# Top-k over folded pairs, and normalisation moved to POOL, in an attention and GELU kernel

## The chip, the cores and the metric

The kernel runs on one core of a Trainium2 chip. The metric is the device time of one launch in microseconds, the median of the runs shown. A core has five engines that matter here, each with its own in-order queue of instructions: PE (TensorE, matrix multiplication), DVE (VectorE), ACT (ScalarE), POOL (GpSimd) and SP, which issues most transfers. The engines wait for one another by semaphores; within one engine the order is the order in which the program emits the instructions.

## What is computed

```python
# q, k, v: (8, 8, 576, 64), w_in: (512, 2048), w_out: (2048, 512), all float32
scores = matmul(q, k.transpose(0, 1, 3, 2)) / sqrt(64)
kth    = np.partition(scores, -32, axis=-1)[..., -32:-31]      # the 32nd largest of a row
scores = np.where(scores >= kth, scores, -1e9)
scores = scores - max(scores, axis=-1)
attn   = exp(scores);  attn = attn / (sum(attn, axis=-1) + 1e-9)
x      = matmul(attn, v)              # brought to (4608, 512): tokens x heads*64
h      = x @ w_in                     # 4608 x 2048
out    = (0.5 * h * (1 + erf(h / sqrt(2)))) @ w_out
```

## The kernel before

**Items.** The 64 heads are taken in pairs (32 pairs), and the rows of a pair in blocks of 128. An item is one block of two rows of scores a partition: `s` is 128 x 1152, two rows of 576 scores (`e` = 0 and 1). Blocks 0 to 3 of a head give one item each, and the last 64 rows of two pairs share an item. There are N = 144 items, 18 a batch.

**The loop.** Iteration n of the main loop (L662) works on several items at once, each a stage further: the scores of item n + 2 (L668: matmuls on PE at L290 and L294, copied out by ACT at L304 and L305), the top-k of item n (L721, on DVE), the softmax of item n - 1 (ACT, L386 and L387), the transposes of item n - 2 (PE, L418 and L436, copied by ACT) and the product with v of item n - 3 (L473). Between them stand pieces of the two large products, at most eight an iteration and four in iterations 10 and 11 (`left`, L664): L525 is the product with w_in, L536 the GELU on ACT, L561 the product with w_out.

**Top-k.** `top_k` (L332) finds the 32 largest of each row on DVE in four rounds. A round takes the eight largest (L347, `max`), and, except the last, replaces these eight by the lowest number (L350, `match_replace`), for both rows in turn. That is 8 maxima and 6 replacements over 576 numbers an item. After the last round a hook runs: the DVE transposes of q and k of a later pair where one is due (L255; each lets SP load that buffer's next pair, six transfers for q and six for k), and `inverse` of item n - 1 (L373, a reciprocal of the softmax sum).

**Threshold and softmax.** `threshold` (L357) is two small POOL operations behind the end of top-k. ACT lowers what is below the 32nd value (Prelu with a steep slope) and exponentiates, summing into `den`. `add_small` (L379) on POOL adds 1e-9 when both rows of item n - 1 are done. `normalise` (L392) multiplies the rows of item n - 1 by `rden`. It is emitted behind the threshold of item n, so it is behind it in POOL's queue. In the iterations where the weights of the next slot are finished by POOL (`on_pool`, slots after START = 10 whose words are already loaded), both multiplications run on DVE instead.

**Weights.** The weights arrive as halves of 64-bit numbers and are put together into float32 in 16 units of 128 x 1024, one in each of the slots 1 to 10 and 13 to 18. `weights_size` makes two or three ACT passes (L190, L192, L194). `weights_add` and `weights_end` are POOL additions (L213, L225), in the late slots with a POOL scaling ahead of them (L210). Most units are staged in the part of `w_out_sb` that is not filled yet, four of them in a pool of their own (`stage`, tile `words`).

**Other names.** `xT` holds the attention output transposed, as a ring of 1152 tokens (`RING`), four groups of features. `keep_busy` (L636) puts matmuls without a use on PE in the first ten iterations. `load` (L88) brings one pair of q, k or v: for q and k six transfers, four of them of the 64 or 72 KB kind and two of the 8 KB kind for the last 64 rows of the second head. Before the loop, L112 to L114 load pair 0 (k from ACT's queue, q from SP's), L628 to L631 load pair 1 and the first weights from SP's queue, and L642 to L647 transpose pairs 0 and 1 on DVE and issue the scores of items 0 and 1.

Of the kernel before, what the change touches and what calls it, by code (L numbers as in the profile page):

```python
# [8 lines left out]
TOPK = 32  # L9
LOWEST = -3.4028234e38  # L10
# [4 lines left out]
def kernel(  # L15
# [69 lines left out]
    def raw_of(n, pair):  # L85
        return raws[n][pair % len(raws[n])]

    def load(n, pair, queue=None, queue2=None):  # L88
        if pair >= n_pairs:
            return  # L90
        queue = queue or nc.sync
        queue2 = queue2 or queue
        b, h0 = pair // NP, 2 * (pair % NP)
        t, src = raw_of(n, pair), sources[n]
        if n != "v":
            for e, a in ((0, 0), (0, 1), (1, 0), (1, 1)):
                at = e * D + a * SQ
                for lo, hi, c in ((0, S, 0),) if e == 0 else ((0, SM, 0), (SM, S, SM + TL)):
                    (queue if a == 0 else queue2).dma_start(  # L99
                        out=t[at : at + SQ, c : c + hi - lo].rearrange("p (j d) -> p j d", d=SQ),  # L100
                        in_=src[b, h0 + e, lo:hi, a * SQ : (a + 1) * SQ].rearrange(
                            "(j p) d -> p j d", p=SQ
                        ),
                    )
            return
        for e in range(2):
            queue.dma_start(
                out=t[:, 0:NM, e, :], in_=src[b, h0 + e, 0:SM].rearrange("(t p) d -> p t d", p=P)
            )
            queue2.dma_start(out=t[e * TL : (e + 1) * TL, NM, e, :], in_=src[b, h0 + e, SM:S])  # L110

    load("k", 0, nc.scalar)  # L112
    load("q", 0)
    make_identity(nc, ident)  # L114


# [36 lines left out]
    def load_weights(n, queue=None):  # L153

        queue = queue or nc.sync
        u = unit_in(n)
        if u is None:
            return
        src, r, c, dst = weights_of(u)
        if src.dtype == f32:  # L160
            for x in range(2):
                queue.dma_start(
                    out=dst[:, x], in_=src[(r + x) * P : (r + x + 1) * P, c : c + WS]
                )
            return


        half, i = src.bitcast(u16), ORDER.index(u)
        if i not in (2, 12, 14, 15):
            at = FT // 2 + 4 * (i % 2)  # L170
            t = w_out_sb[:, at : at + 4, :].rearrange("p (a b) n -> p a (b n)", a=2)
        else:
            t = stage.tile([P, 2, 2 * WS], f32, tag="words", name="words")
        for a in range(2):
            queue.dma_start(
                out=t[:, a].bitcast(u16)[:, 0 : 4 * WS - 1],
                in_=half[(r + a) * P : (r + a + 1) * P, 4 * c + 1 : 4 * (c + WS)],
            )
        words[u] = t

    def parts(u):

        t, dst = words[u], weights_of(u)[3].bitcast(i32)
        return t[:, :, 0::2], t.bitcast(mybir.dt.int16)[:, :, 2::4], t[:, :, 1::2].bitcast(i32), dst

    def weights_size(u):
        if u not in words:
# [12 lines left out]
    def waits(u):  # L200

        return u == ORDER[-1]
# [3 lines left out]
    def weights_add(u):  # L206
        if u in words:
            w, _, below, d = parts(u)
            if on_pool(u):
                nc.gpsimd.tensor_scalar(  # L210
                    w.bitcast(i32), w.bitcast(u32), 2.0**-13, None, op0=ALU.mult
                )
            nc.gpsimd.tensor_tensor(d, d, below, op=ALU.add)  # L213
            if not ends_late(u):
                weights_end(u)
        made.add(u)
# [33 lines left out]
    def transpose_qk(pair):  # L250

        def piece(x, n):
            if pair not in qk_of:
                qk_of[pair] = work.tile([P, 2 * QK], f32, tag="qk", bufs=NP + 2, name="qk")
            nc.vector.transpose(qk_of[pair][:, x * QK : (x + 1) * QK], raw_of(n, pair))  # L255
            load(n, pair + 2)

        return [lambda x=x, n=n: piece(x, n) for x, n in ((1, "k"), (0, "q"))]
# [5 lines left out]
    def row(i, e):  # L264
        return S_of[i][:, e * S : (e + 1) * S]
# [14 lines left out]
    def scores(i):  # L280
# [25 lines left out]
        else:  # L306
# [22 lines left out]
                func=AF.Copy, scale=scale,  # L329
            )  # L330

    def top_k(i, hooks):  # L332


        stat_of[i] = st = {
            "top": work.tile([P, 2, TOPK], f32, tag="top", name="top"),
            "neg": work.tile([P, 2, 2], f32, tag="neg", name="neg"),
            "bias": work.tile([P, 2], f32, tag="bias", name="bias"),
            "den": work.tile([P, 2], f32, tag="den", name="den"),
            "rden": work.tile([P, 2], f32, tag="rden", name="rden"),  # L340
        }
        cur = [row(i, e) for e in range(2)]
        rest = work.tile([P, 2, S], f32, tag="rest", bufs=1, name="rest")
        n_op = 0
        for r in range(TOPK // 8):
            for e in range(2):
                nc.vector.max(st["top"][:, e, 8 * r : 8 * r + 8], cur[e])  # L347
            if r < TOPK // 8 - 1:
                for e in range(2):
                    nc.vector.match_replace(  # L350
                        rest[:, e], st["top"][:, e, 8 * r : 8 * r + 8], cur[e], LOWEST
                    )
                cur = [rest[:, e] for e in range(2)]
            if r in hooks:
                hooks.pop(r)()

    def threshold(i):  # L357

# [30 lines left out]
            accum_out=st["den"][:, e : e + 1],  # L389
        )  # L390

    def normalise(i, on_dve):  # L392

        if i < 0 or i >= N:
            return
        st = stat_of[i]
        for e in range(2):
            s = row(i, e)
            (nc.vector if e >= 2 - on_dve else nc.gpsimd).tensor_scalar(  # L399
                s, s, st["rden"][:, e : e + 1], None, op0=ALU.mult  # L400
            )

    pt_now = [None]
# [218 lines left out]
    ready, left = [0], [0]  # L622

    eager = [False]
    staging = ExitStack()
    stage = staging.enter_context(tc.tile_pool(name="stage", bufs=1))

    load("k", 1)  # L628
    load("q", 1)
    for n in range(1, 3):  # L630
        load_weights(n)  # L631
# [7 lines left out]
            nc.tensor.matmul(warm[:, 0:P], lhsT=m, rhs=m, start=True, stop=True)  # L639

    keep_busy(WARM, idle)
    for pair in range(2):  # L642
        for piece in transpose_qk(pair):
            piece()
        if pair == 0:
            scores(0)
            scores(1)  # L647

# [11 lines left out]
    for n in range(ahead):  # L662

        left[0] = 4 if n in (START, START + 1) else 8  # L664
        eager[0] = n > N
        if not waits(unit_in(n)):
            weights_add(unit_in(n))
        scores(n + 2)  # L668
        product = attend(n - 3)
        late = n > START  # L670
        if n <= START:

            softmax(n - 1, 0)
        copy_x()
        if waits(unit_in(n)):
            weights_size(unit_in(n))
            weights_add(unit_in(n))
        mlp(1)
        tr = transposes(n - 2)
        if product and n > START and done[0] < len(pieces) and pieces[done[0]][0] > ready[0]:  # L680

            for piece in tr[:1]:
                piece()
            tr, ready[0] = tr[1:], n_tok[0]
        if n > START:
            softmax(n - 1, 0)
        mlp(1)
        if not late:
            softmax(n - 1, 1)
        mlp(1)  # L690
        if n < START:

            keep_busy((4 if product or n == 0 else 14) * (1 if n < 5 else 2), ident)
        for piece in tr[:-1]:
            piece()
            if n < START and product and piece is tr[0]:
                keep_busy(5 if n < 5 else 10, ident)
            ready[0] = n_tok[0]
            mlp(1)
        ready[0] = n_tok[0]  # L700
        if late:
            softmax(n - 1, 1)
        add_small(n - 1)
        if ends_late(unit_in(n)):
            weights_end(unit_in(n))
        for piece in tr[-1:]:
            piece()
            mlp(1)
        if n == 1:
            keep_busy(8, ident)  # L710

        run_gelus()
        mlp(left[0])
        run_gelus()
        if n < N:
            def behind_searches():
                for piece in prep_in.pop(n, []):
                    piece()
                inverse(n - 1)

            top_k(n, {3: behind_searches})  # L721
        else:
            inverse(n - 1)
        threshold(n)
        u = unit_in(n + 1)

        normalise(n - 1, 2 if on_pool(u) else 0)

        if not waits(unit_in(n + 1)):
            weights_size(unit_in(n + 1))  # L730
        for m in (n + 1, n + 2):

            if m > 2 and waits(unit_in(m)) == (m == n + 1):
                load_weights(m)
        if n <= NP:
            load("v", n)

    ready[0], left[0] = NT, len(pieces)
    while done[0] < len(pieces):
        mlp(1)  # L740
        run_gelus()
    staging.close()


# [30 lines left out]
```

## Time and profile before

| | us |
|---|---|
| median of 3 runs | 1621.87 (1621.77 to 1622.47) |
| the profiled execution: its own time | 1622.63 |
| its span, first to last instruction | 1620.9 |
| mean granted TensorE clock | 0.987 |
| ACT busy | 1144.1 |
| POOL busy | 663.9 |

The span is what the profile covers; the run's own time is 1.73 us more. PE's busy time is modelled from pipelined matmuls, so a busy PE is not PE at its peak. What an edit is worth depends on the engine that sets the pace at that place, which the chain of waits shows: it starts from the last instruction and goes back, at each step, to what released it.

Single groups that the change touches, from the groups by shape (busy time in us and mean in ns; x is the count):

```profile
L350 DVE MATCH_REPLACE8 rest<-top,rest 128x576 f32<-128x576 f32 x576 | 423.2, 742 | 0.0
L350 DVE MATCH_VALUE_LOAD rest<-top,rest 128x8 f32 x576 | 44.2, 77 | 0.0
L373 DVE RECIPROCAL rden<-den 128x2 f32<-128x2 f32 x144 | 21.6, 150 | 75.1 <-POOL den L379 74.9
L379 POOL TENSOR_SCALAR den<-den 128x2 f32<-128x2 f32 x144 | 32.1, 223 | 785.2 <-ACT s L387 784.8
L399 DVE TENSOR_SCALAR s<-s,rden 128x576 f32<-128x576 f32 x10 | 7.0, 741 | 0.3
```

The last column is the idle time of the engine before these instructions and what ended it. A replacement is two instructions, the load of its eight values and the pass itself.

### The profile page before, as it was taken

To read this page: it belongs to the slowest core of one execution; us is meant where nothing else is said; L and a number is where in the kernel's file an instruction comes from. 1 tells how busy PE (TensorE), PEld (TensorE's weight loads), DVE (VectorE), ACT (ScalarE), POOL (GpSimd) and SP (SyncE) were. 2 spreads that over 40 slices of the span, in tenths; PEclk is the share of its full clock that TensorE was granted. 3 is DMA by queue.
4 is the path that set the end of the run, shared out by engine and by line. 5 is a ranking of instruction groups with operands and counts; after the bars stand their busy time and mean duration, and the time that the engine had idled before them with its cause. 6 is when DMAs were issued, how large, how long until landed. Compare 5 with 4: busy or idle time off the path is not lost.

```text
span 1620.9 us, 25358 instructions
## 1 busy us (share of the span) xinstructions
PE 1588.7 (98%) x8864; PEld 1082.8 (67%) x8864; DVE 1460.1 (90%) x3108; ACT 1144.1 (71%) x2038; POOL 663.9 (41%) x758
## 2 busy tenths in 40 slices
PE   6899899999999999999999999999999999999999
PEld 5676476766666667776666667676666666666665
DVE  7999999999999999999999998999999999999800
ACT  4898787777777777777777777777777777777720
POOL 3886754333444333344333344333344333444400
PEclk7999999999999999999999999999999999999999
DMA  6533320011101211012100111002110101000000
GB/s 138 169 93 93 92 58 1 20 32 36 35 1 32 33 24 29 1 29 44 36 16 16 29 30 43 1 21 37 30 36 8 36 1 36 2 14 7 1 13 13
DMA packets 202640, 56.18 MB, mean 35 GB/s; under 512 B 193680, under 2 KB 193936, under 8 KB 202512
## 3 DMA queue, kind: packets, MB, share of 16 engines
q1 hardware_dynamic: 199968, 54.13, 14.5%
q8 instruction: 70, 1.15, 0.3%
q10 hardware_dynamic: 2544, 0.43, 0.1%
q14 instruction: 58, 0.48, 0.1%
HBM read 45.08 MB, written 9.44 MB: 34 GB/s over the span
## 4 chain that ended last, share of the span: by engine, by line
PE 87%; DVE 10%; DMA 1%; SPq 1%; issue 0%; POOL 0%; ACT 0%; DVEq 0%; ACTq 0%; POOLq 0%
PE y_ps L561 30%; PE h_ps L525 30%; PE o L473 8%; PE s_ps L294 7%; PE tp L436 7%; DVE top L347 5%; DVE rest L350 4%; PE t_ps L290 2%; PE o L484 1%; PE tp_t L418 1%; PE s_ps L321 1%; SPq L99 1%; DVE qk L255 1%; DVE s L399 0%; PE t_ps L310 0%
## 5 line engine op out<-in xcount | busy, mean ns | idle before, releaser
L347 DVE MAX8 top<-rest 128x8 f32<-128x576 f32 x864 | 609.2, 746 | 0.0
L525 PE MATMUL h_ps<-xT,w_in_sb 128*128 128x256 f32 (+1 forms) x2560 | 547.5, 361 | 0.0
L561 PE MATMUL y_ps<-w_out_sb,g 128*128 128x512 f32 x1152 | 545.0, 600 | 0.0
L399 POOL TENSOR_SCALAR s<-s,rden 128x576 f32<-128x576 f32 x278 | 477.1, 1726 | 8.6 <-DVE rden L373 8.0
L525 PEld LDWEIGHTS h_ps<-xT,w_in_sb 128*128 128x128 f32 x2560 | 432.7, 191 | 64.2 <-issue 14.8
L350 DVE MATCH_REPLACE8 rest<-top,rest 128x576 f32<-128x576 f32 x576 | 423.2, 742 | 0.0
L379 POOL TENSOR_SCALAR den<-den 128x2 f32<-128x2 f32 x144 | 32.1, 223 | 785.2 <-ACT s L387 784.8
L561 PEld LDWEIGHTS y_ps<-w_out_sb,g 128*128 128x128 f32 x1152 | 198.8, 191 | 187.0 <-issue 186.2
L304 ACT ACTIVATE s<-s_ps 128x1024 f32<-128x1024 f32 x127 | 130.7, 1029 | 177.4 <-PE s_ps L294 177.0
L387 ACT ACTIVATE s<-s,bias 128x576 f32<-128x576 f32 x288 | 223.3, 776 | 12.6
L386 ACT ACTIVATE s<-s,neg 128x576 f32<-128x576 f32 x288 | 224.1, 778 | 0.5 <-POOL neg L362 0.4
L443 ACT COPY pt<-tp 128x512 f32<-128x512 f32 x256 | 147.1, 575 | 101.9 <-PE tp L436 101.3
L350 DVE MATCH_REPLACE8 rest<-top,s 128x576 f32<-128x576 f32 x288 | 211.6, 742 | 0.0
L436 PEld LDWEIGHTS tp<-ident,s 128*128 128x128 f32 x1152 | 143.5, 142 | 89.3 <-issue 57.6
L347 DVE MAX8 top<-s 128x8 f32<-128x576 f32 x288 | 201.5, 741 | 0.0
L436 PE MATMUL tp<-ident,s 128*128 128x128 f32 x1152 | 174.2, 275 | 3.9 <-ACT pt L419 3.5
L473 PE MATMUL o<-pt,raw_v 128*64 128x256 f32 x1280 | 152.9, 385 | 0.5 <-ACT pt L443 0.5
L294 PE MATMUL s_ps<-qk 64*128 64x256 f32 x1024 | 150.8, 414 | 0.9 <-ACT s L302 0.5
L473 PEld LDWEIGHTS o<-pt,raw_v 128*64 128x64 f32 x1280 | 86.5, 137 | 64.5 <-issue 15.1
L294 PEld LDWEIGHTS s_ps<-qk 64*128 64x128 f32 x1024 | 91.1, 192 | 23.6 <-ACT s L302 0.8
L536 ACT ACTIVATE g<-h_ps 128x512 f32<-128x512 f32 x144 | 78.6, 594 | 37.8 <-PE h_ps L525 37.1
L387 ACT ACT_TABLE_LOAD x67 | 86.0, 1283 | 5.1
(72 smaller groups left out, 1002.9 us busy)
## 6 DMA issues: line engine op xcount, KB each, us to landing
raw_v<-in_v_dram SPq DMA_DIRECT2D x64, 128.0 KB, 2.4
out_dram<-y SPq DMA_DIRECT2D x31, 256.0 KB, 2.2
w_out_sb<-in_moe_w_in_dram SPq DMA_DIRECT2D x14, 511.8 KB, 4.9
w_out_sb<-in_moe_w_out_dram SPq DMA_DIRECT2D x10, 511.8 KB, 4.1
raw_q<-in_q_dram SPq DMA_DIRECT2D x64, 72.0 KB, 2.2
raw_k<-in_k_dram SPq DMA_DIRECT2D x62, 72.0 KB, 2.3
raw_q<-in_q_dram SPq DMA_DIRECT2D x64, 64.0 KB, 2.2
raw_k<-in_k_dram SPq DMA_DIRECT2D x62, 64.0 KB, 2.2
```

The costliest lines, as they stand in the source:

```text
L294: nc.tensor.matmul(s_ps[:, e, c * 256 : (c + 1) * 256], lhsT=lhsT[rows, :], rhs=qk[rows, KM + c * 256 : KM + (c + 1) * 256], start=True, s ...
L304: nc.scalar.activation(spread(s, S + TL, SM), s_ps, func=AF.Copy, scale=scale)
L347: nc.vector.max(st["top"][:, e, 8 * r : 8 * r + 8], cur[e])
L350: nc.vector.match_replace(rest[:, e], st["top"][:, e, 8 * r : 8 * r + 8], cur[e], LOWEST)
L386: nc.scalar.activation(s, s, func=AF.Prelu, bias=st["neg"][:, e, 1:2], scale=1.0, alpha=STEEP)
L387: nc.scalar.activation(s, s, func=AF.Exp, bias=st["bias"][:, e : e + 1], scale=1.0, accum_out=st["den"][:, e : e + 1],)
L399: (nc.vector if e >= 2 - on_dve else nc.gpsimd).tensor_scalar(s, s, st["rden"][:, e : e + 1], None, op0=ALU.mult)
L436: nc.tensor.transpose(tp[:, j * P : (j + 1) * P], s[:, first + j * P : first + (j + 1) * P], ident)
L443: nc.scalar.copy(out=dst, in_=tp.rearrange("p (j n) -> p j n", j=NM))
L473: nc.tensor.matmul(o[e * D : (e + 1) * D, 0:n], lhsT=vt[:, j, e, :], rhs=pt[:, e * NM + j if j < NM else 2 * NM, :], start=(j == 0), stop= ...
L525: nc.tensor.matmul(h_tile(u)[:, i, :], lhsT=w_in_sb[:, ko, f * P : (f + 1) * P], rhs=xT[:, ko, c0 : c0 + n], start=(ko == 0), stop=(ko == ...
L561: nc.tensor.matmul(y_of[sub], lhsT=g_of[u][:, i, sub * P : (sub + 1) * P], rhs=w_out_sb[:, f, :], start=(f == 0), stop=(f == FT - 1),)
```

## The change

- **Top-k over pairs.** `fold` splits a row of 576 into two halves of 288 and takes element by element the larger (`high_of`) and the smaller (`low_of`). The smaller is a DVE minimum up to item 19 (`BY_POOL` = 20). From item 20 it is made on POOL from the bit patterns as integers: sum of both, less the larger. A smaller number can be among the 32 largest only if its partner is, so at most 16 of the 32 come from `low_of`. `top_k` searches the 32 largest of `high_of` (four rounds) and, from the third round, the 16 largest of `low_of` (two rounds), in place. With a_1 to a_32 and b_1 to b_16 falling, the 32nd of both together is the largest over j = 0 to 16 of min(a_(32-j), b_j), with b_0 the greatest number: one minimum over 2 x 17 with one list read backwards, and one reduction.
- **When the fold runs.** Up to item 19 the fold of item n + 1 follows the top-k of item n on DVE. From item 20 it stands at the head of iteration n, on DVE and POOL. Item 0 is folded right before its search.
- **Normalisation** is always on POOL, as multiplication by `rden` and a second one by 1.0. The POOL scaling of the weights (L210) gets a second multiplication by 1.0 as well.
- **First loads.** For pair 0 the two transfers of the last rows go to POOL's queue, for k and for q (`for_tail`), and k of pair 1 goes to ACT's queue. The DVE transposes of pair 1 move from before the loop into the hook behind the first round of item 0's search; the scores of item 2 move behind that search.
- **Staging.** The pool `stage` is gone; its four units are staged in the last 512 tokens of `xT`, in four transfers instead of two.

```diff
-    load("k", 0, nc.scalar)
-    load("q", 0)
+    load("k", 0, nc.scalar, nc.gpsimd)
+    load("q", 0, None, nc.gpsimd)
...
-            t = stage.tile([P, 2, 2 * WS], f32, tag="words", name="words")
-        for a in range(2):
+            t = xT[:, :, RING - WS :]
+        n = 4 * WS // (t.shape[1] // 2)
+        for a in range(t.shape[1]):
...
-                    w.bitcast(i32), w.bitcast(u32), 2.0**-13, None, op0=ALU.mult
+                    w.bitcast(i32), w.bitcast(u32), 2.0**-13, 1.0, op0=ALU.mult, op1=ALU.mult
...
+    def fold(i):
+        if i >= N:
+            return
+        two = S_of[i].rearrange("p (e h n) -> p h e n", e=2, h=2)
+        high_of, low_of = HL_of[i] = [
+            work.tile([P, 2, S // 2], f32, tag=t, name=t) for t in ("high_of", "low_of")
+        ]
+        a, b, hi, lo = (t.bitcast(i32) for t in (two[:, 0], two[:, 1], high_of, low_of))
+        nc.vector.tensor_tensor(high_of, two[:, 0], two[:, 1], op=ALU.max)
+        if i < BY_POOL:
+            nc.vector.tensor_tensor(low_of, two[:, 0], two[:, 1], op=ALU.min)
+            return
+        nc.gpsimd.tensor_tensor(lo, a, b, op=ALU.add)
+        nc.gpsimd.tensor_tensor(lo, lo, hi, op=ALU.subtract)
...
+        def round_of(x, dst, last):
+            for e in range(2):
+                nc.vector.max(dst[:, e], x[:, e])
+            if not last:
+                for e in range(2):
+                    nc.vector.match_replace(x[:, e], dst[:, e], x[:, e], LOWEST)
         for r in range(TOPK // 8):
+            round_of(high_of, top[:, :, 8 * r : 8 * r + 8], r == TOPK // 8 - 1)
+            if r >= TOPK // 16:
+                x = r - TOPK // 16
+                round_of(low_of, low_top[:, :, 8 * x + 1 : 8 * x + 9], r == TOPK // 8 - 1)
             if r in hooks:
                 hooks.pop(r)()
...
+        nc.vector.tensor_tensor(both, rising, low_top, op=ALU.min)
+        nc.vector.tensor_reduce(
+            top[:, :, TOPK - 1 : TOPK], both, axis=mybir.AxisListType.X, op=ALU.max
+        )
...
-            (nc.vector if e >= 2 - on_dve else nc.gpsimd).tensor_scalar(
-                s, s, st["rden"][:, e : e + 1], None, op0=ALU.mult
+            nc.gpsimd.tensor_scalar(
+                s, s, st["rden"][:, e : e + 1], 1.0, op0=ALU.mult, op1=ALU.mult
             )
...
-    load("k", 1)
+    load("k", 1, nc.scalar)
...
-    for pair in range(2):
-        for piece in transpose_qk(pair):
-            piece()
-        if pair == 0:
-            scores(0)
-            scores(1)
+    for piece in transpose_qk(0):
+        piece()
+    scores(0)
+    scores(1)
...
+        if n + 1 >= BY_POOL:
+            fold(n + 1)
...
-        scores(n + 2)
+        if n > 0:
+            scores(n + 2)
...
-            top_k(n, {3: behind_searches})
+            hooks = {3: behind_searches}
+            if n == 0:
+                fold(0)
+                hooks[0] = lambda: [piece() for piece in transpose_qk(1)]
+            top_k(n, hooks)
+            if n == 0:
+                scores(2)
+            if n + 1 < BY_POOL:
+                fold(n + 1)
...
-        normalise(n - 1, 2 if on_pool(u) else 0)
+        normalise(n - 1)
```

More of the change, by code (lines that the diff above doesn't have):

```diff
@@ L86, in raw_of, with load @@
         return raws[n][pair % len(raws[n])]
-    def load(n, pair, queue=None, queue2=None):
+    def load(n, pair, queue=None, for_tail=None):
         if pair >= n_pairs:
@@ L91, in load @@
         queue = queue or nc.sync
-        queue2 = queue2 or queue
+        for_tail = for_tail or queue
         b, h0 = pair // NP, 2 * (pair % NP)
@@ L98, in load @@
                 for lo, hi, c in ((0, S, 0),) if e == 0 else ((0, SM, 0), (SM, S, SM + TL)):
-                    (queue if a == 0 else queue2).dma_start(
+                    (for_tail if lo else queue).dma_start(
                         out=t[at : at + SQ, c : c + hi - lo].rearrange("p (j d) -> p j d", d=SQ),
@@ L109, in load @@
             )
-            queue2.dma_start(out=t[e * TL : (e + 1) * TL, NM, e, :], in_=src[b, h0 + e, SM:S])
-    load("k", 0, nc.scalar)
-    load("q", 0)
+            queue.dma_start(out=t[e * TL : (e + 1) * TL, NM, e, :], in_=src[b, h0 + e, SM:S])
+    load("k", 0, nc.scalar, nc.gpsimd)
+    load("q", 0, None, nc.gpsimd)
     make_identity(nc, ident)
@@ L172, in load_weights @@
         else:
-            t = stage.tile([P, 2, 2 * WS], f32, tag="words", name="words")
-        for a in range(2):
+            t = xT[:, :, RING - WS :]
+        n = 4 * WS // (t.shape[1] // 2)
+        for a in range(t.shape[1]):
+            row, at = divmod(a * n, 4 * WS)
+            end = min(at + n, 4 * WS - 1)
             queue.dma_start(
-                out=t[:, a].bitcast(u16)[:, 0 : 4 * WS - 1],
-                in_=half[(r + a) * P : (r + a + 1) * P, 4 * c + 1 : 4 * (c + WS)],
+                out=t[:, a].bitcast(u16)[:, 0 : end - at],
+                in_=half[(r + row) * P : (r + row + 1) * P, 4 * c + 1 + at : 4 * c + 1 + end],
             )
@@ L183, in parts @@
         t, dst = words[u], weights_of(u)[3].bitcast(i32)
-        return t[:, :, 0::2], t.bitcast(mybir.dt.int16)[:, :, 2::4], t[:, :, 1::2].bitcast(i32), dst
+        if t.shape[1] == 4:
+            t = t.rearrange("p (a b) n -> p a b n", a=2)
+            dst = dst.rearrange("p a (b n) -> p a b n", b=2)
+        return t[..., 0::2], t.bitcast(mybir.dt.int16)[..., 2::4], t[..., 1::2].bitcast(i32), dst
     def weights_size(u):
@@ L330, in scores @@
             )
+    HL_of = {}
+    HALF = TOPK // 2
+    BY_POOL = 2 * START
+    low_tops = [const.tile([P, 2, HALF + 1], f32, name=f"low_top{x}") for x in range(2)]
+    for t in low_tops:
+        nc.vector.memset(t[:, :, 0:1], -LOWEST)
+    def fold(i):
[12 more added lines that the diff above has]
+        nc.gpsimd.tensor_tensor(lo, lo, hi, op=ALU.subtract)
     def top_k(i, hooks):
@@ L341, in top_k @@
         }
-        cur = [row(i, e) for e in range(2)]
-        rest = work.tile([P, 2, S], f32, tag="rest", bufs=1, name="rest")
-        n_op = 0
-        for r in range(TOPK // 8):
[L346 to L353, printed above, removed]
+        top, low_top, (high_of, low_of) = st["top"], low_tops[i % 2], HL_of.pop(i)
+        def round_of(x, dst, last):
[4 more added lines that the diff above has]
+                    nc.vector.match_replace(x[:, e], dst[:, e], x[:, e], LOWEST)
+        for r in range(TOPK // 8):
+            round_of(high_of, top[:, :, 8 * r : 8 * r + 8], r == TOPK // 8 - 1)
+            if r >= TOPK // 16:
+                x = r - TOPK // 16
+                round_of(low_of, low_top[:, :, 8 * x + 1 : 8 * x + 9], r == TOPK // 8 - 1)
             if r in hooks:
                 hooks.pop(r)()
+        both = work.tile([P, 2, HALF + 1], f32, tag="both", bufs=1, name="both")
+        falling = top[:, :, HALF - 1 :]
+        rising = bass.AP(
+            tensor=falling.tensor, offset=falling.offset + HALF,
+            ap=[list(falling.ap[0]), list(falling.ap[1]), [-1, HALF + 1]],
+        )
+        nc.vector.tensor_tensor(both, rising, low_top, op=ALU.min)
+        nc.vector.tensor_reduce(
+            top[:, :, TOPK - 1 : TOPK], both, axis=mybir.AxisListType.X, op=ALU.max
+        )
     def threshold(i):
@@ L390, in softmax, with normalise @@
         )
-    def normalise(i, on_dve):
+    def normalise(i):
         if i < 0 or i >= N:
@@ L624 @@
     eager = [False]
-    staging = ExitStack()
-    stage = staging.enter_context(tc.tile_pool(name="stage", bufs=1))
-    load("k", 1)
+    load("k", 1, nc.scalar)
     load("q", 1)
@@ L741 @@
         run_gelus()
-    staging.close()
 _INS = ["q", "k", "v", "moe_w_in", "moe_w_out"]
```

## The prediction

> **What bounds the kernel now.** I read four views in this order: busy times and slices, the chain of waits from the start to 260 us, the windows of single items, and the groups by shape with a close timeline.
>
> ```profile
> span 1620.9 us, 25358 instructions
> PE 1588.7 (98%) x8864; PEld 1082.8 (67%) x8864; DVE 1460.1 (90%) x3108; ACT 1144.1 (71%) x2038; POOL 663.9 (41%) x758
> PE   6899899999999999999999999999999999999999
> DVE  7999999999999999999999998999999999999800
> ```
>
> PE and DVE both look full, so shares settle nothing; the order in time does.
>
> ```profile
> 10.49 1.77 DMA raw_q<-in_q_dram
> ...
> 13.16 1.37 DVE top L347 x2
> 14.53 1.46 DVE rest L350 x2
> 15.98 1.32 DVE top L347 x2
> ...
> 145.20 1.65 DVE s L399 x2
> ...
> 191.68 0.74 DVE qk L255
> 192.48 0.48 PE t_ps L310 x4
> ```
>
> The chain is DVE from 13.16 to 192.4 us (items 0 to 16) and PE without a gap from there to the end. Matmul work after 192 us is not touched, so only what shortens or lengthens items 0 to 16 moves the end. An item begins where its first maximum begins: 13.16, 23.60, 34.01, 44.36, 54.86, 64.57 and so on; 9.71 us when nothing else is on DVE. Two maxima start 1.32 apart and two replacements 1.46, so an instruction costs 0.66 and 0.73, and 8 x 0.66 + 6 x 0.73 = 9.66, plus 0.05 for the reciprocal.
>
> ```profile
> 83.97:93.67 9.70, 9.61 (x83) 8.44 (x81) 9.70 (x23) 9.38 (x15) 9.29 (x8) 1.00 0.35 111
> 134.66:146.85 12.19, 12.19 (x68) 9.31 (x65) 12.08 (x25) 11.98 (x21) 5.95 (x6) 1.00 0.49 119
> 169.83:182.03 12.20, 11.97 (x67) 6.72 (x67) 12.16 (x26) 8.15 (x12) 8.41 (x7) 1.00 0.55 135
> ```
>
> Columns: window and its length, then busy time of PE, weight load, DVE, ACT and POOL with counts. Up to item 10 ACT (9.38 of 9.70) and POOL (9.29) stand just behind DVE: a faster DVE alone wins at most 0.3 us an item there. Items 12 to 16 last 12.19, 10.77, 12.21, 12.20 and 12.17 us, together 59.5, against 10.76 that PE needs for an item when it sets the pace (score matmuls at 238.66 and 249.42 us in the chain).
>
> **The change, part by part.**
>
> *Searches on 288.* The 8-value load before a replacement takes 0.067, a 576 maximum 0.66, so 0.593 / 568 = 1.04 ns an element. At 288 a maximum is 0.66 - 0.30 = 0.36 and a replacement 0.43. There are now 12 and 8: 4.32 + 3.44 = 7.76. The fold adds a maximum and, up to item 19, a minimum over 576 pairs in all; the nearest row is the 576 maximum, so 2 x 0.66 = 1.32. The closing minimum over 34 and the reduction are like the reciprocal (0.15 for 2 elements) plus 34 ns, each waiting for the one before: 0.43. Sum 7.76 + 1.32 + 0.43 + 0.05 = 9.56 against 9.71: 0.15 us an item, nearly nothing. From item 20 the minimum is POOL's and DVE saves 0.8, but PE sets the pace there, so I cost that at nothing. POOL's two integer operations on 576 are 2 x 1.35 (128x1024 took 2.41) = 2.7 us, hidden in the wait of POOL for ACT before its small addition (784.8 us in 139 times, 5.6 each); with that cover gone an item could lose up to 2.7 less DVE's 0.8.
>
> *Contention of the fold with POOL.* No two-input DVE operation exists before. The nearest rows are the ten normalisations on DVE, which meet POOL:
>
> ```profile
> 180.16 2.94 POOL L210 TENSOR_SCALAR w_out_sb<-w_out_sb 128x1024 int32<-128x1024 uint32 x1
> 180.31 1.72 DVE L399 TENSOR_SCALAR s<-s,rden 128x576 f32<-128x576 f32 x2
> 156.67 0.95 DVE L399 TENSOR_SCALAR s<-s,rden 128x576 f32<-128x576 f32 x2
> ```
>
> Where POOL was already running, the pair took 1.72; where DVE came first, 0.95 (POOL's next operation then took 3.23 instead of 2.95). So a stall is worth 0.78 for DVE; bounds per item 0 and 2 x 0.78 = 1.56. The fold starts right behind the reduction on which POOL's threshold waits, so DVE comes first: I take 0.2. Items 1 to 11: (0.2 - 0.15) x 11 = +0.6; ends -1.7 and +15.5.
> The Trainium skill, "SBUF — State Buffer", section "Who interferes with whom", speaks against this part: an instruction with two SBUF inputs contends with a GpSimd instruction that reads, and the loser blocks fully. By the rule a late fold would wait out a whole normalisation of 1.73 us, near +17 us over these 11 items; the pair of 1.72 us finished while POOL's 2.94 ran on, which is less than that.
>
> *Normalisation.* DVE loses ten instructions in items 12 to 16: 1.65 + 0.95 + 1.01 + 1.72 + 1.69 = 7.0 us. POOL gets them, and all carry a second multiplication, as does the weight scaling.
>
> ```profile
> L399 POOL TENSOR_SCALAR s<-s,rden 128x576 f32<-128x576 f32 x278 | 477.1, 1726 | 8.6 <-DVE rden L373 8.0 <-PE o L473 0.4
> L213 POOL TENSOR_TENSOR w_in_sb<-w_in_sb,w_out_sb 128x1024 int32<-128x1024 int32 x7 | 16.9, 2411 | 0.2
> masks.py:199 POOL TENSOR_SCALAR_AFFINE_SELECT ident<-ident 128x128 f32<-128x128 f32 x1 | 0.3, 293 | 0.1
> ```
>
> A one-multiplication pass costs (1726 - 223) / 574 = 2.6 ns an element (223 is the 128x2 row), more than the two-input addition at 2.1; the affine select, with two computations, costs (293 - 223) / 126 = 0.56. So the slow row is not bound by reading. Bounds for two multiplications on 576: 0.54 by the select, 3.2 by twice the present work. I take 1.1, midway between the select and the present row, since in having both operations filled the select is nearer and in everything else the present row is. The scaling on 1024 then goes from 2.95 to about 1.9.
> The Trainium skill, "GPSIMD Engine Reference", section "Elementwise — side-by-side cycle accounting", puts a body of at most two operations at 1.03 cycles an element: an estimate of 0.5 us and the fixed cost, 0.7; no row of a scaling here is that fast.
>
> *Items 12 to 16.* DVE: 5 x 9.56 + 3.72 for transposes + 5 x 0.2 = 52.5. POOL: 1.9 + 2 x 2.41 + 2.2 + 0.65 for the small ones + 0.7 of gaps = 10.3 an item. PE: 5 x 10.76 = 53.8, the largest: 5.7 saved. One thing comes due: the scalar engine waited 2.44 us at 179.08 for a weight transfer issued behind twelve q and k transfers; a shorter item lengthens that wait, and the staged words take four issues instead of two (0.43 each more). I take off 1.2: -4.5. Bounds: -6.5 and, with POOL as slow as now, the rival below.
>
> *The start.* k and q each move two of six issues to POOL's queue (0.6 each on ACT: six took 3.62), pair 1 comes from ACT and SP side by side, so its transposes no longer hold item 0 back (the wait below). Item 0's scores are complete at 11.91 now, by d earlier then; fold 1.37, searches 7.76, tail 0.43, transposes 1.5 + 0.75 put item 1 at 23.8 - d, against 23.60. No transfer from POOL is in the trace. At ACT's 0.6 and 2.3 to land, the four land at 5.7 and d is 1.1; at twice the issue cost q comes at 8.05 instead of 7.12, d = -0.9. I take 0.6: -0.4; ends -0.9 and +1.1.
>
> ```profile
> 12.39 0.85 DVE L255 STREAM_TRANSPOSE qk<-raw_q 128x640 f32<-128x640 f32 x1 [2.16 <-DMA raw_q<-in_q_dram]
> ```
>
> SP gets weights and v earlier by the six k issues; scores of item 2 fall behind item 0's search, with a whole item to spare. Staging in the unused end of xT is free: that part is first written after item 20.
>
> **Sum.** -0.4 + 0.6 - 4.5 = -4.3 us. The profiled execution took 1622.63 with a span of 1620.9; the span becomes 1616.6, and against the median of 1621.87 the time is **1617.6 us**.
>
> **Rivals.**
> *POOL becomes the bound* (slower). If two multiplications cost what one does, POOL holds the loop in items 12 to 16: threshold 0.43 + normalisation 3.45 + weights 7.77 + addition 0.22 + gaps 0.7, then reciprocal and tail 0.58: 13.15 an item, 65.8 against 59.5. -0.4 + 0.6 + 6.2: 1628.3. It decides from about 1.4 us a pass. For it: the present row; against it: the select. At 3.2 a pass items 3 to 11 go too: 9.3 + 2.95 against 9.71, 23 us, and 5.9 more in each of the five, 29.
> *The fold stalls on POOL* (slower). One stall of 0.78 an item: (0.78 - 0.15) x 11 = 6.9, and items 12 to 16 win 2.9: 1625.5; two stalls: about 1637. It decides from 0.55 an item. For it: the 1.72 pair; against it: who comes first.
> *The gain is taken back by ACT*, which is busy 11.98 of 12.19 in item 12, and by the late transfer: items 12 to 16 win 1 us and the search is no shorter than claimed above: about 1621.1. Against it: ACT averages 10.0 over the five.
>
> **How the numbers follow.** Forecast 0.58, POOL bound 0.15, fold stalls 0.13, ACT 0.14. The forecast alone spans 1612 to 1620: -0.9 - 1.7 - 6.5 at best, 2.5 us worse than the sum at worst. Up to the one-stall and the POOL case the range is 1611 to 1629; beyond it lie two stalls and a dear pass, about 0.1. A measurement tells 0.2% from no change, 3.2 us. Faster: 0.55 of the forecast's 0.58. Same: 0.03 of it, ACT's 0.14, 0.01 of the stalls: 0.18. Slower: 0.15 + 0.12 = 0.27.
>
> **What would show it.** Right: normalisations on POOL near 1.1 us; item length about 9.8 up to item 11; the chain passing from DVE to PE at item 12 instead of 17; maxima of 288 each 0.36 apart. Wrong: normalisations at 1.7 or more with DVE waiting for the small addition in items 12 to 16; folds of 1.2 us or more before item 20; first transposes after 7.1 us; PE idle after 200 us, which would overturn the claim that nothing there counts.

## The result, and the profile after

The changed kernel takes 1616.53 us (median; 1614.95 to 1618.04) against 1621.87 (1621.77 to 1622.47): a ratio of 0.9967, 95% interval 0.9954 to 0.9979. That is 5.3 us less where 4.3 were forecast. The profiled execution took 1615.54 us with a span of 1613.8. The time came close to the forecast, but two terms of the sum were too small and one that I had put at nothing was not nothing. They cancelled in part: that the number came this near is partly luck.

The page of the changed kernel: span, busy time by engine, and the slices of PE and DVE.

```profile
span 1613.8 us, 27225 instructions
PE 1585.1 (98%) x8864; PEld 1083.1 (67%) x8864; DVE 1336.8 (83%) x4704; ACT 1143.0 (71%) x2038; POOL 803.2 (50%) x1020
PE   7889999999999999999999999999999999999999
DVE  8999978888889988888988888888888888888700
```

DVE is 123 us less busy and POOL 139 us more, and the end moved by 7 us only: from item 17 on PE set the pace already, so DVE's saving there is idle time.

The groups by shape (busy time, mean ns, idle before):

```profile
L440 POOL TENSOR_SCALAR s<-s,rden 128x576 f32<-128x576 f32 x288 | 212.3, 748 | 0.4 <-DVE rden L414 0.4
L375 DVE MAX8 top<-high_of 128x8 f32<-128x288 f32 x1152 | 467.5, 447 | 0.0
L354 DVE TENSOR_TENSOR high_of<-s 128x576 f32<-128x576 f32 x144 | 107.8, 749 | 1.9 <-ACT s L308 1.9
L403 POOL TENSOR_SCALAR neg<-top 128x4 f32<-128x4 f32 x144 | 94.2, 654 | 116.5 <-DVE top L394 116.5
L216 POOL TENSOR_SCALAR xT<-xT 128x1024 int32<-128x1024 uint32 x3 | 3.4, 1134 | 1.8 <-DMA xT<-in_moe_w_out_dram 1.7
```

A normalisation with two multiplications takes 748 ns on POOL where one took 1726, a weight scaling 1134 where one took 2.95 us. The folds take 0.75 us on DVE and are never held up (the longest took 0.76), but the first operation of POOL's threshold, which runs beside them, takes 654 ns instead of 231.

The chain of waits of the changed kernel, from the start to 260 us (start, length, what):

```profile
10.68 0.76 DVE high_of L354
...
62.05 1.64 DVE both L393
...
190.69 2.40 POOL w_out_sb L231
194.46 3.78 DMA xT<-in_moe_w_out_dram
198.35 1.23 ACT w_out_sb L196
199.60 1.23 ACT xT L198
200.96 2.90 PE h_ps L566 x6
```

Two things in it were not in the forecast: a closing minimum of 1.64 us at 62 us (item 4), and a piece around 200 us in which PE waits for a weight unit that is staged in `xT`.

To see where time was won and lost, I compare the reciprocal of each search in both kernels (it stands at the end of each item on DVE):

| end of the search of item | before | after | lead | won in between |
|---|---|---|---|---|
| 1 | 33.89 | 32.09 | 1.80 | start and items 0, 1: 1.80 |
| 12 | 144.96 | 142.48 | 2.48 | items 2 to 12: 0.68 |
| 17 | 203.77 | 193.44 | 10.33 | items 13 to 17: 7.85 |
| 20 | 237.08 | 230.41 | 6.67 | items 18 to 20: -3.66 |

From there both go at PE's pace (10.6 us an item on average) and the lead stays (7.2 us at the last reciprocal). (The reciprocal in search n belongs to item n - 1; the five searches with DVE normalisations behind them are 12 to 16.)

### The profile page after: what moved, and what is told of

Read it like the earlier page. It is cut to its first block, busy times and chain, and to the rows that moved or that the text cites. A ratio compares the mean times of both kernels' runs of the same rounds, so it can differ in the third digit from the quotient of the medians.

```text
span 1613.8 us, 27225 instructions
## 1 busy us (share of the span) xinstructions
PE 1585.1 (98%) x8864; PEld 1083.1 (67%) x8864; DVE 1336.8 (83%) x4704; ACT 1143.0 (71%) x2038; POOL 803.2 (50%) x1020
## 4 chain that ended last, share of the span: by engine, by line
PE 88%; DVE 8%; DMA 2%; POOL 1%; SPq 1%; ACT 1%; issue 0%; DVEq 0%; POOLq 0%; ACTq 0%
PE y_ps L602 30%; PE h_ps L566 30%; PE o L514 8%; PE s_ps L300 7%; PE tp L477 7%; DVE top L375 2%; DVE high_of L378 2%; PE t_ps L296 2%; PE o L525 1%; DVE low_top L375 1%; PE tp_t L459 1%; PE s_ps L327 1%; DVE qk L261 1%; DMA w_out_sb<-in_moe_w_in_dram 1%; DVE low_of L378 1%; DVE high_of L354 0%
## 5 line engine op out<-in xcount | busy, mean ns | idle before, releaser
L375 DVE MAX8 top<-high_of 128x8 f32<-128x288 f32 x1152 | 467.5, 447 | 0.0
L378 DVE MATCH_REPLACE8 high_of<-top,high_of 128x288 f32<-128x288 f32 x864 | 376.1, 443 | 0.0
L375 DVE MAX8 low_top<-low_of 128x8 f32<-128x288 f32 x576 | 232.6, 446 | 0.0
L440 POOL TENSOR_SCALAR s<-s,rden 128x576 f32<-128x576 f32 x288 | 212.3, 748 | 0.4 <-DVE rden L414 0.4
L477 PEld LDWEIGHTS tp<-ident,s 128*128 128x128 f32 x1152 | 143.3, 141 | 89.1 <-issue 58.8
L359 POOL TENSOR_TENSOR low_of<-low_of,high_of 128x576 int32<-128x576 int32 x124 | 174.8, 1410 | 9.7
L414 DVE RECIPROCAL rden<-den 128x2 f32<-128x2 f32 x144 | 22.7, 158 | 187.5 <-POOL den L420 187.5
L358 POOL TENSOR_TENSOR low_of<-s 128x576 int32<-128x576 int32 x124 | 175.6, 1416 | 0.0
L403 POOL TENSOR_SCALAR neg<-top 128x4 f32<-128x4 f32 x144 | 94.2, 654 | 116.5 <-DVE top L394 116.5
```

The lines of the kernel that those rows point to most:

```text
L358: nc.gpsimd.tensor_tensor(lo, a, b, op=ALU.add)
L359: nc.gpsimd.tensor_tensor(lo, lo, hi, op=ALU.subtract)
L375: nc.vector.max(dst[:, e], x[:, e])
L378: nc.vector.match_replace(x[:, e], dst[:, e], x[:, e], LOWEST)
L440: nc.gpsimd.tensor_scalar(s, s, st["rden"][:, e : e + 1], 1.0, op0=ALU.mult, op1=ALU.mult)
L477: nc.tensor.transpose(tp[:, j * P : (j + 1) * P], s[:, first + j * P : first + (j + 1) * P], ident)
```

## Experiments

The theories: A, the gain is the ten normalisations that leave DVE; B, the shorter search; C, the start; D, the staging in `xT` takes part of it back. Each diff is against the kernel named.

**The changed kernel once more.**

> The changed kernel unchanged, for a second profile. Its first profile showed one stall of 1.5 us (the closing minimum of item 4 waiting for a POOL addition) and score matmuls of item 0 at full clock (1.13 us for eight instead of 2.08 before). If these are part of the change, both are here again and the time is 1616.5 within 1. If they are chance, one or both are gone, and the runs scatter over 1615 to 1618 as they did.

1616.79 us (1615.56 to 1617.13), ratio 0.9962 (0.9950 to 0.9975). The stall of item 4 and the wait at 200 us are here again. The short first score matmuls are not. The timeline of the first and of the second profile:

```profile
8.38 1.13 PE L300 MATMUL s_ps<-qk 64*128 64x256 f32 x8
```

```profile
8.66 2.08 PE L300 MATMUL s_ps<-qk 64*128 64x256 f32 x8
```

The same eight matmuls take 1.13 or 2.08 us, and the lead at the reciprocal of item 1's search is 1.80 or 0.56. So 1.2 us of the start is chance: 0.95 by these matmuls and 0.28 by their start. From 8 to 10 us the granted clock is 0.94 in the first profile, and 0.50 in the kernel before, where the eight take 2.08 us too. The second profile has no record of the clock before 24 us, so a low clock there is not shown.

**The normalisations alone** (against the kernel before).

```diff
-                    w.bitcast(i32), w.bitcast(u32), 2.0**-13, None, op0=ALU.mult
+                    w.bitcast(i32), w.bitcast(u32), 2.0**-13, 1.0, op0=ALU.mult, op1=ALU.mult
...
-            (nc.vector if e >= 2 - on_dve else nc.gpsimd).tensor_scalar(
-                s, s, st["rden"][:, e : e + 1], None, op0=ALU.mult
+            nc.gpsimd.tensor_scalar(
+                s, s, st["rden"][:, e : e + 1], 1.0, op0=ALU.mult, op1=ALU.mult
```

> The kernel before with the second multiplication and all normalisations on POOL, nothing else. Theory A (the gain is the ten normalisations that DVE loses in items 12 to 16): DVE's items 12 to 16 become 7 us shorter, PE takes over at item 12 to 13 instead of 17, 4 to 5 us faster than before, about 1617.5. Theory B (the gain is the shorter search): at most 1 us faster, above 1621. Theory C (the gain is the start): no change, 1621.9.

1613.29 us (1613.28 to 1613.56), ratio 0.9943 (0.9930 to 0.9955): 8.5 us won by two lines, more than by the whole change and about twice what theory A said. The windows of three items of it (columns as before: length, PE, weight load, DVE, ACT, POOL):

```profile
144.91:154.59 9.68, 9.68 (x45) 4.52 (x45) 9.68 (x23) 8.89 (x16) 7.69 (x6) 1.00 0.74 215
154.59:165.77 11.18, 11.18 (x77) 8.51 (x73) 11.18 (x24) 10.99 (x17) 8.55 (x10) 1.00 0.07 30
176.20:186.63 10.43, 10.32 (x63) 7.87 (x59) 10.43 (x24) 10.28 (x16) 8.12 (x8) 1.00 0.45 129
```

DVE is still busy all the time; the five items took 51.4 us instead of 58.8, and the lead of 8.75 at item 20 is kept to the end. Theory A stands, and the rest of the change must cost 3.2 us.

Why twice as much? The chain of waits passes from DVE to PE here:

```profile
186.71 0.06 DVE rden L373
186.76 0.33 PE t_ps L310 x4
```

That is 5.7 us before the 192.48 us of the kernel before. The two spans differ by 9.4 us, so 3.7 us more are won behind this point, where the same matmuls are left. The kernel before comes to it after an idle time of PE, and runs on at half the clock (the timeline, and three windows, whose first number behind the engines is PE's granted clock):

```profile
192.48 0.48 PE L310 MATMUL t_ps<-qk 128*64 128x64 f32 x4 [2.90 <-DVE rden L373]
192.00:194.00 2.00, 1.52 (x12) 0.60 (x12) 1.97 (x4) 0.00 (x0) 1.84 (x2) 0.51 0.22 35
194.00:196.00 2.00, 2.00 (x10) 0.68 (x3) 2.00 (x5) 1.05 (x2) 1.92 (x2) 0.50 0.64 104
196.00:198.00 2.00, 2.00 (x4) 0.83 (x3) 2.00 (x5) 1.67 (x4) 1.92 (x2) 0.50 0.05 8
```

Its clock is back at 1.00 at 198.88 us; 6.4 us at half the clock cost 3.2, an estimate. In the kernel with the normalisations alone PE does not wait there, and the clock stays at 1.00.

**The second multiplication, with the ten normalisations left on DVE** (against the kernel before: the same, except that DVE's branch stays).

> The kernel before with the second multiplication wherever POOL scales, but the ten normalisations of items 12 to 16 left on DVE. Theory A says that POOL's speed alone wins nothing, since POOL did not set the pace: within 1 us of before. If POOL's share (9.3 of 9.7 us in items 6 to 10) held the loop through the small additions, 2 us or more are won here. A pass on POOL should take 0.75 us as in the changed kernel if the second multiplication is what makes it fast.

1627.85 us, ratio 1.0034 (1.0022 to 1.0047): 6 us slower, which neither theory expected. The timeline:

```profile
145.11 1.14 POOL L210 TENSOR_SCALAR w_out_sb<-w_out_sb 128x1024 int32<-128x1024 uint32 x1
145.33 3.78 DVE L400 TENSOR_SCALAR s<-s,rden 128x576 f32<-128x576 f32 x2
146.33 2.47 POOL L213 TENSOR_TENSOR w_in_sb<-w_in_sb,w_out_sb 128x1024 int32<-128x1024 int32 x1
```

DVE's pair, 0.95 us where it came first and 1.72 beside the slow scaling, takes 3.78: one instruction waits for the scaling to end (146.25), the next through the whole addition (148.8). In four of the five pairs an instruction takes 2.63 us in this way. The slow scaling had let DVE in; the fast one and the addition do not. So the second multiplication and the move of the normalisations belong together.

**The start alone** (against the kernel before: loads, transposes of pair 1 and scores of item 2 as in the change).

> The kernel before with the first loads, the transposes of pair 1 and the scores of item 2 reordered as in the change, nothing else. Theory C (the 1.8 us that the changed kernel is ahead at the first reciprocal come from this order): item 1 begins 1 us earlier or more, 1.5 us faster. If they come from the clock of the first matmuls by chance, item 1 begins less than 0.7 us earlier when the eight score matmuls take 2.08 us, and the time is within 0.7 of before.

1622.27 us, ratio 0.9998 (0.9989 to 1.0007), the reciprocal in item 1's search ahead by 0.58 us. Theory C falls.

**The normalisations with the staging in `xT`** (the first of these kernels, and the staged words as in the change).

> The kernel before with the second multiplication, all normalisations on POOL (1613.3 so far) and, new, the four staged units in the unused end of xT as in the change. Theory D (the matmuls of the product with w_in wait for the writes of the staged words, because both touch xT; the changed kernel shows one such wait of 2.8 us at 198 us and half the clock behind it): the same wait of PE is here, 4 us slower than without, about 1617.5. If the staging is free, as my prediction said, 1613.3.

1616.64 us (1615.73 to 1617.43), ratio 0.9966 (0.9954 to 0.9979): 3.3 us slower than the normalisations alone, about what the change lacks. Its timeline (the bracket is idle time and what ended it):

```profile
201.78 1.21 ACT L198 ACTIVATE xT<-xT,high 128x1024 int32<-128x1024 int16 x1
203.14 1.53 PE L531 MATMUL h_ps<-xT,w_in_sb 128*128 128x256 f32 x6 [2.56 <-ACT xT L198]
```

The product with w_in, which reads other tokens of `xT`, waits until ACT has written the staged words. In this profile the clock stays at 1.00 behind the wait, and the lead at item 20 is 2.6 us less than without the staging, about the wait itself. The changed kernel has the same wait (2.77 us), and pays for it twice; its windows:

```profile
198.00:200.00 2.00, 0.19 (x1) 0.00 (x0) 2.00 (x8) 1.62 (x2) 1.11 (x1) 1.00 0.01 4
200.00:202.00 2.00, 1.04 (x3) 0.89 (x4) 2.00 (x8) 1.96 (x4) 1.10 (x1) 0.72 0.00 0
202.00:204.00 2.00, 2.00 (x7) 1.53 (x6) 0.99 (x3) 1.91 (x3) 1.92 (x2) 0.50 0.04 8
```

After the idle time PE's granted clock is 0.72, then 0.50, and the six matmuls behind the wait take 2.90 us where six took 1.53 above. That the wait covers tokens it need not, because the staged view reaches over all four feature groups and so over a range of addresses with other tokens in it, is my reading of the code; it was not tried by itself. That the wait comes with the staging is shown by the next two runs.

**The change with its own staging** (against the changed kernel; one buffer for the halves makes the room).

```diff
-            t = xT[:, :, RING - WS :]
+            t = stage.tile([P, 2, 2 * WS], f32, tag="words", name="words")
...
-    BY_POOL = 2 * START
+    BY_POOL = N
...
-            work.tile([P, 2, S // 2], f32, tag=t, name=t) for t in ("high_of", "low_of")
+            work.tile([P, 2, S // 2], f32, tag=t, bufs=1, name=t) for t in ("high_of", "low_of")
```

> The changed kernel with its staging in a pool of its own again; to make room the folded halves have one buffer instead of two and DVE makes the smaller numbers for all items, right behind the search. Theory D: no wait of PE for staged words, PE takes over earlier, 1610 to 1612, below both the changed kernel and the kernel with the normalisations alone. Rival E (the fold costs the 3.3 us by holding up POOL's threshold, 0.65 instead of 0.23 us, and by its stall): 1616 to 1617, as the changed kernel.

1611.62 us (1611.03 to 1612.69), ratio 0.9935 (0.9922 to 0.9948). No wait of PE for staged words is left, and the chain passes to PE in item 12 and stays there:

```profile
147.33 0.33 PE tp_t L453
147.66 0.86 PE y_ps L596 x2
```

Theory D stands; this kernel is 10.3 us faster than the one before.

**Its control: one buffer and DVE folds, staging still in `xT`.**

> Control for the kernel with its own staging: the changed kernel with one buffer for the folded halves and DVE folds for all items, but the staged words still in xT. If the staging alone made the 4.9 us between 1616.5 and 1611.6, this is 1616.5 within 1 and PE waits for the staged words at 198 us as before. If the DVE folds or the single buffer made part of it, the time lies between.

1616.80 us (1614.87 to 1617.15), ratio 0.9961 (0.9947 to 0.9975), as the changed kernel. PE waits 3.20 us for the staged words, and the clock is at 0.50 for 6.8 us around the end of that wait. So the 5 us are the staging's; who makes the smaller numbers from item 20 on changes nothing.

**Normalisations and the start, no fold, own staging.**

> The kernel before with the second multiplication, all normalisations on POOL and the new order of the start; search and staging as before. The start alone changed nothing (1622.3 against 1621.8), so 1613.3 within 0.7. If the start needs a POOL that is not slow, 1 to 2 us less; if it is what costs the changed kernel its 3.3 us, 1616.5.

1612.92 us (1612.39 to 1613.21), ratio 0.9942 (0.9929 to 0.9955). Against the kernel with the fold besides, 1.3 us, with intervals that overlap: a worth of the fold is not shown, and if there is one, it is about that.

**The fold alone** (against the kernel before: DVE folds, one multiplication, ten normalisations on DVE, own staging).

> The kernel before with the fold alone (DVE folds, one buffer, staging in its own pool, one multiplication, ten normalisations on DVE). Theory B (the shorter search wins 0.25 us an item by itself): 2.5 us less up to item 11, 3 to 4 us in all, 1618. If POOL, at 9.3 of 9.7 us an item, cannot follow once the fold holds its threshold up by 0.75 us, nothing is won or some is lost: 1621 to 1625, with the reciprocal waiting for the small addition before item 11.

1643.93 us, ratio 1.0135 (1.0121 to 1.0149): 21 us slower. Up to item 20 it loses 3 us (POOL cannot follow, as the second guess said); the other 18 come later, at PE's pace, where I had put the cost at nothing, and neither guess had them. Two lines of its waits, over the whole span (us in total, times, longest), and the same two of the kernel before:

```profile
PEld tp_t L453 <- POOL s L434: 60.3, 62, 4.2
PE tp_t L453 <- POOL s L434: 17.3, 15, 1.8
```

```profile
PEld tp_t L418 <- POOL s L399: 10.8, 14, 4.0
PE tp_t L418 <- POOL s L399: 4.6, 2, 3.6
```

The fold makes the two operations of the threshold longer by 0.8 us together (664 and 549 ns in the median, instead of 231 and 196), the slow normalisation (3.43 us for two rows) ends later by it, and PE's transposes wait for it. By my reading, PE's pace was covered by less than that.

**The fold amid the search.**

```diff
+            if 0 < n and n + 1 < BY_POOL:
+                hooks[1] = lambda: fold(n + 1)
             top_k(n, hooks)
...
-            if n + 1 < BY_POOL:
+            if n == 0:
                 fold(n + 1)
```

> The changed kernel with the fold of items 2 to 19 moved from behind the search of the item before into the middle of that search (after its second round), when POOL is in a weight addition of 2.4 us. Rival F (a DVE operation with two inputs waits until POOL's running operation ends, as the closing minimum of item 4 did for 1.5 us): the maximum takes 1.5 to 3 us instead of 0.75 in items 2 to 10, 8 to 20 us slower, 1625 to 1637; POOL's small threshold is back at 0.23 us. If DVE only shares the port, the folds stay near 0.75 and the time within 2 us of the changed kernel.

1635.64 us, ratio 1.0082 (1.0068 to 1.0097), 19 us slower than the changed kernel. The timeline:

```profile
48.27 2.39 POOL L219 TENSOR_TENSOR w_in_sb<-w_in_sb,xT 128x1024 int32<-128x1024 int32 x1
49.32 1.96 DVE L354 TENSOR_TENSOR high_of<-s 128x576 f32<-128x576 f32 x1
```

The maximum ends at 51.28, 0.62 us after POOL's addition (50.66): it waited for that. Nine maxima take 1.96 to 1.99 us, and in the items with a weight scaling five minima take 2.95; that is 22 us more than at 0.75 each, about what this kernel has lost by item 20. POOL's threshold is back at 0.23 in these items. The rival "the fold stalls on POOL" is real. What saves the change is the fold's place right behind the reduction, where POOL has nothing running.

**The change with one multiplication.**

> The changed kernel with a single multiplication in both POOL scalings, as before the change (normalisations still all on POOL). By the rival of my prediction POOL then holds the loop in items 12 to 16 at 13.2 us an item: about 10 us slower than the changed kernel or more, 1626 to 1629, one pass 1.73 us and the reciprocal waiting for the small addition. If POOL's pass length does not matter for the gain, 1616.5.

1641.93 us, ratio 1.0122 (1.0106 to 1.0139): 25 us slower than the changed kernel, more than the rival's 12. Items 12 to 18 take 13.6 to 14.7 us each: my 13.15 was near, but it holds seven items, not five, and the transposes wait for POOL afterwards too.

**The weight addition behind the normalisation** (against the change with its own staging).

```diff
-        if ends_late(unit_in(n)):
-            weights_end(unit_in(n))
...
         normalise(n - 1)
+        if ends_late(unit_in(n)):
+            weights_end(unit_in(n))
```

> The changed kernel with its staging in its own pool and DVE folds (1611.6 so far), and the last weight addition of slots 1 to 10 moved behind the normalisation in POOL's queue, so that POOL is idle when the closing minimum runs. If the 2.3 us stall of item 4 (the minimum took 2.42 us in that kernel) is a wait for that addition, the largest minimum is below 0.3 us and the time 2 us less, 1609.5. If the time is set elsewhere by then, 1611.6.

The stall of item 4 in the changed kernel was this (timeline):

```profile
61.23 2.40 POOL L231 TENSOR_TENSOR w_in_sb<-w_in_sb,w_out_sb 128x1024 int32<-128x1024 int32 x1
62.02 1.66 DVE L393 TENSOR_TENSOR both<-top,low_top 128x34 f32<-128x34 f32 x1
```

A minimum over 34 numbers waits for POOL's addition, 63.63, and ends at 63.68. Moving the addition takes the stall away: the largest minimum falls from 2418 ns to 198 (shortest, median, longest, in ns):

```profile
L387 DVE TENSOR_TENSOR both<-top,low_top x144: 159/175/198, 23.1 to 1524.5; 128x34 f32<-128x34 f32 x144
```

But the time is 1611.19 us (1609.71 to 1613.12), ratio 0.9935 (0.9921 to 0.9949), not told apart from 1611.62. The lead of 1.8 us that it has at item 5 is used up by item 18 (207.79 against 207.75 us): past that point PE decides, and what DVE wins ahead of it is lost.

## Why the prediction was right, and where its steps failed

- **What bounds the kernel**: right in part. DVE's 123 us less of work is worth next to nothing from item 17 on. But the sign that I had named, the chain passing from DVE to PE at item 12, shows only with the staging in a pool of its own (147.33 us); in the changed kernel PE has the chain for good from 200.96 us, later than the 192.48 of the kernel before, and PE stands idle just before, which I had named as a sign of being wrong. "Only what shortens or lengthens items 0 to 16 moves the end" left out the clock: 3.7 us of what the normalisations won lie behind item 16.
- **Normalisation, 1.1 us a pass**: right in direction, the size was off. It is 0.748, and 1.13 instead of 1.9 for the scaling; the affine select's 0.54 was the better neighbour. The Trainium skill, "GPSIMD Engine Reference", section "Elementwise — side-by-side cycle accounting", gives 1.03 cycles an element for a body of at most two operations; the estimate of 0.7 from it was nearest. The row of one multiplication, 1.73, does not follow that figure.
- **Items 12 to 16, -4.5**: the mis-sized term. DVE won 7.85 us. I had set PE's steady 10.76 us an item as a floor; it is no floor here. PE did these five in 51.4 us in the kernel with the normalisations alone and in 51.0 in the changed kernel, 10.2 each, with DVE busy for 50.2 us of the 51.0 and PE for 50.4. The 1.2 us for the late weight transfer did not come within these items either.
- **Searches on 288**: right. Maxima start 0.36 apart, replacements 0.43; an item with nothing else on DVE is 9.43 to 9.63 us, 0.1 to 0.3 less than before, where 0.15 less was worked out before contention.
- **Contention, 0.2 an item**: mis-sized the other way round. The fold pays nothing; the closing minimum, of 34 numbers, paid 1.5 us once. Together the items up to 12 of the table gave -0.7 instead of +0.6. The Trainium skill, "SBUF — State Buffer", section "Who interferes with whom", says that the loser blocks fully; the minimum that ended with POOL's addition and the fold of 1.96 us agree, and the 1.72 pair that I held against it is the exception of the slow one-multiplication scaling.
- **The start, -0.4**: about right, 0.6 us of lead, which alone is not seen in the time. Of the 1.8 us in the profile, 1.2 are chance.
- **"Staging in the unused end of xT is free"**: wrong, and the step that failed. It costs 3.3 us without the fold and 5 with it: a wait of PE of 2.56 to 3.20 us, with half the clock behind it in three of four profiles, that the forecast never looked for, because I asked when the tokens are first written and not what else waits on the tile.
- **From item 20 on, nothing**: right for the change, where the shorter pass covers the later threshold; the fold alone, with the long pass, loses 18 us there.

So -0.4 + 0.6 - 4.5 became about -1.8 - 0.7 - 7.85 + 3.7 in the profiled execution.

## What to carry to other kernels

Ask of each part of a large change whether it is the part that wins: two lines won 8.5 us here, and the rest gave back 3. A buffer in a free corner of a tile that others read can bring waits with it, so look for who else waits on that tile. Put a DVE operation with two inputs where POOL is idle, and remember that an edit costed at nothing behind another engine is covered only by a margin: here it was less than 0.8 us, by my reading.

## What was not expected of the hardware

- A POOL multiplication by one factor takes 2.3 to 2.6 times as long as one by two factors (1726 against 748 ns on 128x576, 2.95 against 1.13 us on 128x1024).
- What POOL runs decides what a DVE operation beside it pays: the slow scaling cost a DVE pair 0.78 us, the fast scaling and the addition behind it 2.8.
- A wait of PE can cost more than its length. After idle times of 2.75 to 3.20 us the granted clock is 0.50 for 3.4 to 6.8 us (the kernel before, the changed kernel twice, its control with one buffer). The length alone does not decide: with ten normalisations left on DVE the half clock follows an idle time of 2.17 us at 149 us and does not follow one of 2.38 at 188 us; behind the 2.56 us of the normalisations with the staging in `xT` it does not come either.
- Eight equal matmuls at 8 us took from 1.13 to 2.08 us, with the new start and with the old (1.18 us in one kernel). Where the clock is on record, it falls to 0.50 at 7.73 us in the kernel before (2.08 us), at 8.79 in the change with its own staging (1.75) and at 9.74 in the changed kernel (1.13). The Trainium skill, "TensorE: Matmul & The Clock Gate", section "Part 1: The HAM clock gate (the "warmup" mystery)", says that the ramp varies from run to run because its window runs freely; the 1.13 and 2.08 us in the two profiles of the changed kernel agree with the first half, and no run here shows the window.
